# A fused causal convolution and gated feed-forward on one NeuronCore: reordering the loads and casts of the opening

## The chip, the cores and the metric

The kernel runs on one core of a Trainium2 chip. The metric is the device time of one execution in microseconds: 731.14 us is the median of three runs of the kernel before (730.99 to 731.43). The profile comes from a further execution of 730.78 us, whose profiled span is 728.7 us. All times of single instructions are counted from the start of that span.

Names used here: PE is TensorE (PEld its weight loads), DVE is VectorE, ACT is ScalarE, POOL is GpSimd, SP is SyncE, which here issues DMAs and carries a few waiting no-ops. A "q" behind a name (SPq, ACTq) is the sequencer of the engine.

## The reference: what is computed

Two steps. A causal depthwise convolution of 7 taps along the sequence, with one softmax-normalised set of taps for each of 8 heads of 24 channels; then a feed-forward layer whose activation is h cos h.

```python
def _attn_ref(x, weight):                 # x: (8, 4096, 192), weight: (8, 7)
    w = np.exp(weight - np.max(weight, axis=-1, keepdims=True))
    w = w / (np.sum(w, axis=-1, keepdims=True) + 1e-09)
    x_pad = np.concatenate([np.zeros((B, pad, D)), x], axis=1)       # pad = 6
    idx = np.arange(S)[:, None] + np.arange(K)[None, :]
    x_unf = x_pad[:, idx, :].reshape(B, S, K, H, group)
    return np.einsum('hk,bskhg->bshg', w, x_unf).reshape(B, S, D)

def _moe_ref(x, w_in, w_out):             # x: (32768, 192), w_in: (192, 2048), w_out: (2048, 192)
    h = x @ w_in
    return (h * np.cos(h)) @ w_out
```

All inputs and the output are float32; the kernel multiplies in bfloat16 and adds in float32.

## The kernel before

The 32768 tokens are 64 tiles of 512 (t = 0 to 63) and 32 units of 1024 (a unit is two tiles). A unit goes this way: load x (768 KB, and 96 KB of "edges", the rows ahead of each block of 128), cast to bf16 (GpSimd), convolve on TensorE with a band matrix, copy out of PSUM to `ct`, double it (GpSimd), turn it with a DMA transpose into `cT`, mend the edges (GpSimd). A tile then has eight steps j: `mm1` (h = w_in' cT, 4 matmuls), `gcu` (cosine on ACT, product on DVE), and matmuls `mm2_step` with w_out for tiles one and two behind. The order on each engine is written by hand.

Loads of the opening, all on the queue of SP except the tiny convolution weights:

```python
    w_f = consts.tile([128, NC, NP, 128], FP32)
    w_src = moe_w_in.rearrange("(m k) (t f) -> t m k f", k=NC, t=2)
    HP = NP // 2                                  # NP = 8, NC = 3

    def load_w(q):                                # q: half of the steps j; t: partitions 0-63 or 64-127
        for t in range(2):
            nc.sync.dma_start(out=w_f[64 * t : 64 * t + 64, :, q * HP : (q + 1) * HP, :].rearrange("p k j f -> p k (j f)"),
                              in_=w_src[t, :, :, q * HP * 128 : (q + 1) * HP * 128])

    load_unit(0, 0, NB)                           # blocks 0-3 of unit 0
    load_w(0)
    load_unit(0, NB, UB)                          # blocks 4-7 of unit 0
    load_w(1)
    load_unit(1)
    load_edges(1)
    ...
    def load_wo(q):
        return [nc.sync.dma_start(out=wo_f[:, q * HP : (q + 1) * HP, i], in_=wo_src[:, q * HP : (q + 1) * HP, i])
                for i in range(2)]
```

Casts and the band matrix. `three` deals small copies out to DVE, ACT and POOL in turn; the activation with `AF.Sin` on a scrap cell is there to load the sine table early:

```python
    keep_warm(17)                                 # matmuls on zeros
    ...
    cast_unit(0, 0, NB)                           # ACT; every other cast_unit is GpSimd's
    nc.scalar.activation(out=scrap, in_=one, func=AF.Sin)
    ...                                           # prod, diag (DVE)
    three = [nc.vector.tensor_copy, nc.scalar.copy, nc.gpsimd.tensor_copy]
    for i in range(16):
        q, rows = divmod(i, 4)
        three[i % 3](out=band[...], in_=diag[32 * q : 32 * q + 32])
    for k in range(NC):
        three[(k + 2) % 3](out=w[:, k, 0:HP], in_=w_f[:, k, 0:HP])
    cast_unit(0, NB, UB)
    for q in range(2):
        for dma in load_wo(q):                    # w_out's loads wait for the cast just above
            tc.add_manual_dep(dma.ins, bf_last[0].ins.name, sync_dep, reason="the bandwidth is for what is needed sooner")
    ...
    conv_first()                                  # unit 0, blocks 0-3: convolution, ct copies (L299)
    turn_first(0)                                 # turned by TensorE
    turn_first(1)
    cast_unit(1)
    load_unit(2)
    load_edges(2)
```

A convolution part (`conv_part`) takes two row halves on one PSUM bank; the second group of matmuls waits for a no-op on SP that waits for the first:

```python
        mm(0, 0, start=True)
        mm(2, 1, start=True)
        turn = Turn()
        turn.mark(mm(1, 0), mm(3, 1))             # a nop on SP waits for these
        yield
        turn.wait(mm(2, 0), mm(0, 1))             # these wait for the nop
        ...
```

The order of TensorE and ACT in the first two tiles (h: mm1, r: rest of unit 0's convolution, d1 d2 and c1 c2: the two groups of a convolution part, m: mm2 steps, s: gcu, e: copy of a convolution part; d and c belong to unit 1 in tile 0 and to unit 2 in tile 1):

```python
    PE_FIRST = ["h0a h0b h1 r d1 h2 d2 h3 h4 h5 h6 c1 h7 c2 p m12",
                "h0 m8 h1 m12 q h2 h3 h4 m4 d1 m8 d2 h5 m8 h6 c1 m8 c2 h7 m4 p m8"]
    ACT_FIRST = ["s0a s0b s1 s2 ed1 ed2 s3 s4 s5 s6 ec1 ec2 s7", "s0 s1 s2 s3 s4 ed1 ed2 s5 s6 ec1 ec2 P s7"]
    ...
                if (t, k) == (0, "d1"):
                    turn_unit(0, NB, UB)          # DMA transpose of unit 0, blocks 4-7
                    nc.gpsimd.tensor_copy(out=w[:, :, HP:NP], in_=w_f[:, :, HP:NP])
                    for q in range(2):
                        nc.gpsimd.tensor_copy(out=wo[:, q * HP : (q + 1) * HP], in_=wo_f[:, q * HP : (q + 1) * HP])
    ...
                if t == 1:                        # at "q"
                    turn_unit(1)
                    mend_edges(1)
    ...
        if t == 0:
            double_unit(1)
            load_unit(3)
            load_edges(3)
            cast_unit(2)
        if t == 1:
            double_unit(2)
            cast_unit(3)
```

Of the kernel before, what the change touches and what calls it, by code (L numbers as in the profile page):

```python
# [10 lines left out]
AF = mybir.ActivationFunctionType  # L11
# [5 lines left out]
def kernel(  # L17
# [8 lines left out]
    nc = tc.nc  # L26
# [15 lines left out]
    NC = D // 64  # L42
    R = G // NC
# [24 lines left out]
    def load_edges(u):  # L68
        nc.sync.dma_start(out=x_tiles[u][:, UB, :],
                          in_=xf[u * U - 8 : u * U - 8 + U, :].rearrange("(n t) d -> n t d", t=128)[:, 0:16, :])  # L70

    def load_unit(u, n0=0, n1=UB):
        if n0 == 0:
            x_tiles[u] = xin.tile([128, UB + 1, D], FP32, name="x_f")
        nc.sync.dma_start(out=x_tiles[u][:, n0:n1, :],
                          in_=xf[u * U + n0 * 128 : u * U + n1 * 128, :].rearrange("(n p) d -> p n d", p=128))


    w_f = consts.tile([128, NC, NP, 128], FP32)
    w_src = moe_w_in.rearrange("(m k) (t f) -> t m k f", k=NC, t=2)  # L80
    HP = NP // 2

    def load_w(q):
        for t in range(2):
            nc.sync.dma_start(out=w_f[64 * t : 64 * t + 64, :, q * HP : (q + 1) * HP, :].rearrange("p k j f -> p k (j f)"),  # L85
                              in_=w_src[t, :, :, q * HP * 128 : (q + 1) * HP * 128])

    load_unit(0, 0, NB)
    load_w(0)
    load_unit(0, NB, UB)  # L90
    load_w(1)
    load_unit(1)
    load_edges(1)
    wo_f = consts.tile([128, NP, 2, D], FP32)
    wo_src = moe_w_out.rearrange("(i j p) d -> p j i d", i=2, p=128)

    def load_wo(q):
        return [nc.sync.dma_start(out=wo_f[:, q * HP : (q + 1) * HP, i], in_=wo_src[:, q * HP : (q + 1) * HP, i])
                for i in range(2)]


    one = consts.tile([128, 1], FP32)
# [16 lines left out]
    scrap = consts.tile([128, 1], FP32)  # L119
# [36 lines left out]
    w = consts.tile([128, NC, NP, 128], BF16)  # L156
# [3 lines left out]
    sync_dep = mybir.DependencyInfo(mybir.DependencyClass.Sync, mybir.DependencyReason.DATA)  # L160
# [12 lines left out]
                tc.add_manual_dep(m.ins, self.nop.ins.name, sync_dep, reason="row halves on one bank")  # L173


    bf, bf_last = {}, {}

    def cast_unit(u, n0=0, n1=UB + 1):
        copy = nc.scalar.copy if u == 0 and n0 == 0 else nc.gpsimd.tensor_copy
        bf[u] = xb0 if u == 0 else xbf_pool.tile([128, UB + 1, D], BF16, name="x_bf")  # L180

        o = 1 if u == 0 else 0
        bf_last[u] = copy(out=bf[u][:, n0 + o : n1 + o, :].rearrange("p n (h k r) -> p (n h) k r", k=NC, r=R),  # L183
             in_=x_tiles[u][:, n0:n1, :].rearrange("p n (h r k) -> p (n h) k r", k=NC, r=R))
        if u and u % UPS == 0:
            nc.gpsimd.memset(bf[u][0:8, UB, :], 0.0)
        bf.pop(u - 2, None)
# [56 lines left out]
    def double_unit(u, n0=0, n1=UB + 1):  # L244
        ct = ct_tiles[u]
        nc.gpsimd.tensor_copy(out=ct[:, n0:n1, :, 1, :], in_=ct[:, n0:n1, :, 0, :])  # L246

    def turn_unit(u, n0=0, n1=UB + 1):
        ct = ct_tiles.pop(u)
        if u not in cT:  # L250
            cT[u] = cT_pool.tile([128, UB + 1, NC, 128], BF16, name="cT")
        nc.sync.dma_start_transpose(out=cT[u][:, n0:n1].rearrange("p n c k -> p (n c) k"),  # L252
                                    in_=ct[:, n0:n1].rearrange("p n c t k -> p (n c t k)"))
        cT.pop(u - 2, None)

    def mend_edges(u):

        nc.gpsimd.tensor_copy(out=cT[u][:, 0:UB, :, 0 : K - 1],  # L258
                              in_=cT[u][:, UB].rearrange("p c (n t) -> p n c t", t=16)[:, :, :, 8 : 8 + K - 1])


    cast_unit(0, 0, NB)
    nc.scalar.activation(out=scrap, in_=one, func=AF.Sin)

    prod = consts.tile([128, HQ, E, K], BF16)
    nc.vector.tensor_tensor(out=prod, in0=mask.rearrange("p (o e) k -> p o e k", o=1).to_broadcast([128, HQ, E, K]),
# [4 lines left out]
    three = [nc.vector.tensor_copy, nc.scalar.copy, nc.gpsimd.tensor_copy]  # L271
    for i in range(16):
        q, rows = divmod(i, 4)
        three[i % 3](out=band[32 * rows : 32 * rows + 32, HQ * q : HQ * (q + 1), 32 * rows : 32 * rows + E],
                     in_=diag[32 * q : 32 * q + 32])
    for k in range(NC):
        three[(k + 2) % 3](out=w[:, k, 0:HP], in_=w_f[:, k, 0:HP])
    cast_unit(0, NB, UB)
    for q in range(2):
        for dma in load_wo(q):  # L280
            tc.add_manual_dep(dma.ins, bf_last[0].ins.name, sync_dep, reason="the bandwidth is for what is needed sooner")

    ct_tiles[0] = ct_pool.tile([128, UB + 1, NC, 2, 64], BF16, name="ct")
    cT[0] = cT_pool.tile([128, UB + 1, NC, 128], BF16, name="cT")
    copies = [nc.scalar.copy, nc.vector.tensor_copy]
# [95 lines left out]
    def evac(t, b):  # L381
        if b == 0:
            o_sb[t] = opool.tile([128, NB, D], FP32, name="o_sb")
        nc.scalar.copy(o_sb[t][:, 2 * b : 2 * b + 2, :].rearrange("p s d -> p (s d)"), o_ps.pop((t, b))[:, 0 : 2 * D])  # L384

    def store(t, b0=0, b1=2):
        nc.sync.dma_start(out=out[t * T + b0 * 256 : t * T + b1 * 256, :].rearrange("(n p) d -> p n d", p=128),
                          in_=o_sb[t][:, 2 * b0 : 2 * b1, :])
# [15 lines left out]
    for t in range(NT + 2):  # L404
        u, second = divmod(t, TPU)
        cu, cc = (u + TPU, second) if t >= TPU else (1 + t, 1)
        conv = {"c": conv_part(cu, cc, ring_banks if t else o_banks) if cu < NU else iter(())}
        if t < TPU:
            conv["d"] = conv_part(cu, 0, ring_banks if t else o_banks)
        act, done, h = (ACT_ORDER if t > 1 else ACT_FIRST[t]).split(), set(), {}  # L410

        def flush():
            while act:
                k = act[0]
                need = {"P": "p", "Q": "q", "e": k[1:2] + "2"}.get(k[0], "h" + k[1:])
                if need not in done:
                    return
                act.pop(0)
                if k == "P" and 0 <= t - 1 < NT:
                    evac(t - 1, 0)  # L420
                elif k == "Q" and 0 <= t - 2 < NT:
                    evac(t - 2, 1)
                elif k[0] == "e":
                    next(conv[k[1]], None)
                elif k[0] == "s" and t < NT:
                    gcu(t, int(k[1]), h.pop(k[1:]), *HALVES[k[2:]])

        for k in (PE_ORDER if t > 1 else PE_FIRST[t]).split():
            if k[0] == "h" and t < NT:
                h[k[1:]] = mm1(t, int(k[1]), *HALVES[k[2:]])  # L430
            elif k[0] in conv:
                next(conv[k[0]], None)
                if (t, k) == (0, "d1"):
                    turn_unit(0, NB, UB)
# [3 lines that stand above are left out]
            elif k == "r":  # L438
                conv_rest()
                double_unit(0, NB, UB)  # L440
            elif k[0] == "m":
                for q in range(step, step + int(k[1:])):
                    mm2_step(q)
                step += int(k[1:])
            elif k[0] == "p":
                assert step % (2 * STEPS) == 0
            elif k[0] == "q":
                assert step % (2 * STEPS) == STEPS
            done.add(k)
            flush()  # L450

            if k == "q":
                if second == 0 and t and u + 1 < NU:
                    turn_unit(u + 1)
                    mend_edges(u + 1)
                if t == 1:
                    turn_unit(1)
                    mend_edges(1)
                if second == 0 and u + 3 < NU:
                    cast_unit(u + 3)  # L460
                if second == 1 and t > 1 and cu < NU:
                    double_unit(cu)
                if t == NT + 1:
                    store(NT - 1, 1, 2)
            if k == "p":
                if t < NT + 1 and 0 <= t - 2:
                    store(t - 2)
                if t == NT:
                    store(NT - 1, 0, 1)
                if second == 1 and u + 4 < NU:  # L470
                    load_unit(u + 4)
                    load_edges(u + 4)
# [4 lines that stand above are left out]
            cast_unit(2)  # L477
        if t == 1:
            double_unit(2)
            cast_unit(3)  # L480


# [28 lines left out]
```

## Time and profile before

| | before |
|---|---|
| time, median of 3 runs | 731.14 us |
| profiled span | 728.7 us |
| TensorE busy | 711.5 us (98%) |
| ACT, DVE, GpSimd busy | 618.1, 611.2, 151.3 us |
| two tiles in the steady part | 22.0 us |
| tile 1's first mm1 matmul starts | 30.07 us |
| tile 2's first convolution matmul starts | 46.37 us |
| HBM read and written | 31.36 and 25.17 MB |

How to read it: busy time is a sum over the whole span, and a stage of some 45 us, in which the pipeline fills, is hardly seen in it. The timeline and the busy time of short stretches show that stage. In a timeline line, the bracket gives the idle time of the engine ahead of the instruction and what released it. A DMA issued on SP shows only the time that its issue took; when its data had landed is seen from the instruction that waited for it.

### The profile page before, as it was taken

To read this page: it belongs to the slowest core of one execution; us is meant where nothing else is said; L and a number is where in the kernel's file an instruction comes from. 1 tells how busy PE (TensorE), PEld (TensorE's weight loads), DVE (VectorE), ACT (ScalarE), POOL (GpSimd) and SP (SyncE) were. 2 spreads that over 40 slices of the span, in tenths; PEclk is the share of its full clock that TensorE was granted. 3 is DMA by queue.
4 is the path that set the end of the run, shared out by engine and by line. 5 is a ranking of instruction groups with operands and counts; after the bars stand their busy time and mean duration, and the time that the engine had idled before them with its cause. 6 is when DMAs were issued, how large, how long until landed. Compare 5 with 4: busy or idle time off the path is not lost.

```text
span 728.7 us, 26373 instructions
## 1 busy us (share of the span) xinstructions
PE 711.5 (98%) x11848; PEld 531.9 (73%) x11848; DVE 611.2 (84%) x535; ACT 618.1 (85%) x782; POOL 151.3 (21%) x126
## 2 busy tenths in 40 slices
PE   6789999999999999999999999999999999999997
PEld 3467777777777777777777777777777777777776
DVE  5568888888988888888888888888888888888884
ACT  5678889888888888888888888888888988888883
POOL 4622222102222111222202222211222211221000
PEclk9899999999999999999999999999999999999999
DMA  9863445654435554445654344555454555333411
GB/s 211 192 129 104 110 95 143 143 123 111 117 89 133 143 139 105 113 95 121 143 143 106 110 104 112 142 143 106 116 111 96 144 142 122 111 76 81 85 46 66
DMA packets 184081, 86.04 MB, mean 118 GB/s; under 512 B 111648, under 2 KB 183200, under 8 KB 183968
## 3 DMA queue, kind: packets, MB, share of 16 engines
q1 hardware_dynamic: 183960, 84.36, 48.3%
q8 instruction: 92, 1.51, 0.8%
q14 instruction: 21, 0.17, 0.1%
q10 hardware_dynamic: 8, 0.00, 0.0%
HBM read 31.36 MB, written 25.17 MB: 78 GB/s over the span
## 4 chain that ended last, share of the span: by engine, by line
PE 93%; DMA 2%; POOL 2%; issue 1%; SPq 1%; ACT 0%; DVE 0%; DVEq 0%; POOLq 0%
PE o_ps L372 45%; PE h L342 44%; PE h L194 3%; DMA x_f<-in_x_dram 1%; DMA wo_f<-in_moe_w_out_dram 1%; POOL x_bf L183 1%; SPq L252 1%; PE h L372 0%; POOL wo L437 0%; ACT cs L349 0%; POOL w L435 0%; SPq L85 0%; DVE g L353 0%; DVEq L506 0%; POOL ct L246 0%
## 5 line engine op out<-in xcount | busy, mean ns | idle before, releaser
L353 DVE TENSOR_TENSOR g<-h,cs 128x1024 bf16<-128x1024 f32 (+1 forms) x513 | 603.5, 1218 | 102.3 <-ACT cs L349 97.7
L349 ACT ACTIVATE cs<-h 128x1024 bf16<-128x1024 f32 (+1 forms) x513 | 511.8, 1026 | 65.8 <-PE h L342 58.4
L372 PE MATMUL o_ps<-wo,g 64*128 64x192 bf16 x8128 | 423.7, 243 | 1.8 <-ACT ct L209 0.6
L372 PEld LDWEIGHTS <-g 64*128 64x128 bf16 x8192 | 362.1, 94 | 85.6 <-SPq L167 1.2
L342 PE MATMUL h<-cT,w 64*128 64x512 bf16 (+1 forms) x3078 | 400.9, 378 | 0.9 <-DVE cT L310 0.3
L342 PEld LDWEIGHTS <-w 64*128 64x128 bf16 x3078 | 155.6, 94 | 87.6 <-issue 4.3
L258 POOL COPY cT<-cT 128x144 bf16<-128x144 bf16 x31 | 9.5, 308 | 497.6 <-DMA cT<-ct 366.2
L183 POOL CAST x_bf<-x_f 128x1728 bf16<-128x1728 f32 (+1 forms) x32 | 80.6, 2518 | 6.9 <-DMA x_f<-in_x_dram 6.9
L209 ACT CAST ct<-h 128x432 bf16<-128x432 f32 x120 | 56.4, 522 | 29.8 <-PE h L194 28.5
L384 ACT COPY o_sb<-o_ps 128x384 f32<-128x384 f32 x127 | 60.1, 473 | 5.0 <-PE o_ps L372 5.0
L246 POOL COPY ct<-ct 128x1728 bf16<-128x1728 bf16 (+1 forms) x32 | 51.2, 1601 | 25.3 <-ACT ct L209 24.4
L194 PE MATMUL h<-x_bf,band 64*128 64x216 bf16 x480 | 43.0, 254 | 2.0 <-POOL x_bf L183 1.2
L194 PEld LDWEIGHTS <-band 64*128 64x128 bf16 (+1 forms) x512 | 22.4, 94 | 12.6 <-issue 8.7
L194 PE MATMUL o_ps<-x_bf,band 128*128 128x96 bf16 (+1 forms) x32 | 2.7, 260 | 6.4 <-POOL x_bf L183 6.4
L110 PE MATMUL o_ps<-zero 128*128 128x512 bf16 x20 | 6.5, 488 | 1.3 <-DVE zero L105 1.3
L372 PE MATMUL h<-wo,g 64*128 64x192 bf16 x64 | 5.8, 243 | 0.0
L110 PEld LDWEIGHTS <-zero 128*128 128x128 bf16 x20 | 2.1, 116 | 4.3 <-issue 1.9
L437 POOL CAST wo<-wo_f 128x1536 bf16<-128x1536 f32 x2 | 2.9, 1472 | 0.0
L209 ACT CAST ct<-o_ps 128x432 bf16<-128x432 f32 (+1 forms) x6 | 2.4, 457 | 0.3 <-PE o_ps L194 0.3
L120 ACT ACT_TABLE_LOAD x1 | 1.3, 1283 | 1.4 <-PEq L495 1.4
L384 ACT COPY o_sb<-h 128x384 f32<-128x384 f32 x1 | 0.5, 479 | 2.4 <-PE h L372 2.4
L183 ACT CAST x_bf<-x_f 128x768 bf16<-128x768 f32 x1 | 1.2, 1243 | 1.1 <-DMA x_f<-in_x_dram 1.1
(48 smaller groups left out, 28.6 us busy)
## 6 DMA issues: line engine op xcount, KB each, us to landing
out_dram<-o_sb SPq DMA_DIRECT2D x63, 384.0 KB
x_f<-in_x_dram SPq DMA_DIRECT2D x31, 768.0 KB
x_f<-in_x_dram SPq DMA_DIRECT2D x31, 96.0 KB
w_f<-in_moe_w_in_dram SPq DMA_DIRECT2D x4, 384.0 KB
wo_f<-in_moe_w_out_dram SPq DMA_DIRECT2D x4, 384.0 KB
x_f<-in_x_dram SPq DMA_DIRECT2D x2, 384.0 KB
cT<-ct SPq DMA_TRANSPOSE x32
out_dram<-o_sb SPq DMA_DIRECT2D x2, 192.0 KB
```

The lines of the kernel that those rows point to most:

```text
L110: nc.tensor.matmul(out=idle, lhsT=zero[:, 0:128], rhs=zero, start=True, stop=True)
L183: bf_last[u] = copy(out=bf[u][:, n0 + o : n1 + o, :].rearrange("p n (h k r) -> p (n h) k r", k=NC, r=R), in_=x_tiles[u][:, n0:n1, :].rearr ...
L194: return nc.tensor.matmul(out=ps[i // 2][:, 0 : (n1 - n0) * 2 * G].rearrange("p (n k i r) -> p i n k r", n=n1 - n0, k=NC, i=2)[:, i % 2], ...
L209: copy(o[:, :, 0, :], i[:, :, 0, :])
L246: nc.gpsimd.tensor_copy(out=ct[:, n0:n1, :, 1, :], in_=ct[:, n0:n1, :, 0, :])
L252: nc.sync.dma_start_transpose(out=cT[u][:, n0:n1].rearrange("p n c k -> p (n c) k"), in_=ct[:, n0:n1].rearrange("p n c t k -> p (n c t k)"))
L258: nc.gpsimd.tensor_copy(out=cT[u][:, 0:UB, :, 0 : K - 1], in_=cT[u][:, UB].rearrange("p c (n t) -> p n c t", t=16)[:, :, :, 8 : 8 + K - 1])
L342: nc.tensor.matmul(out=h[:, i, n0 * 128 : n1 * 128], lhsT=w[rows, k, j, :], rhs=c[rows, m0 + n0 : m0 + n1, k, :], start=(k == 0), stop=(k ...
L349: nc.scalar.activation(out=cs[:, :, part], in_=h[:, :, part], func=AF.Sin, bias=math.pi / 2.0, scale=1.0)
L353: nc.vector.tensor_tensor(out=g_tiles[t][:, 2 * j : 2 * j + 2, part], in0=h[:, :, part], in1=cs[:, :, part], op=ALU.mult)
L372: m = nc.tensor.matmul(out=o_ps[tt, b][:, si * D : (si + 1) * D], lhsT=g_tiles[tt][rows, f, s * 128 : (s + 1) * 128], rhs=wo[rows, f // 2, ...
L384: nc.scalar.copy(o_sb[t][:, 2 * b : 2 * b + 2, :].rearrange("p s d -> p (s d)"), o_ps.pop((t, b))[:, 0 : 2 * D])
```

## The change

It rearranges the opening and leaves what is computed, and the work of the steady part, as it is:

- The two row halves of w_in's first half are issued by two queues, SP's and ACT's.
- Unit 1 and its edges are issued ahead of w_in's second half.
- The four loads of w_out follow in the same queue at once; the explicit wait for the cast of unit 0's second half is gone.
- The scrap activation that loads the sine table stands behind ACT's band copies instead of ahead of them.
- The three casts of w_in's first half go to DVE (k = 0) and GpSimd (k = 1, 2), none to ACT.
- The cast of unit 3 stands, in GpSimd's order, between the transpose and the edge mending of unit 1 at "q" of tile 1, instead of behind the doubling of unit 2 at the end of tile 1.

Its purpose is to have what the first tiles need land and be cast in the order in which it is needed.

```diff
-    def load_w(q):
+    def load_w(q, queues):
         for t in range(2):
-            nc.sync.dma_start(out=w_f[64 * t : 64 * t + 64, ...
+            queues[t].dma_start(out=w_f[64 * t : 64 * t + 64, ...
     load_unit(0, 0, NB)
-    load_w(0)
+    load_w(0, [nc.sync, nc.scalar])
     load_unit(0, NB, UB)
-    load_w(1)
     load_unit(1)
     load_edges(1)
+    load_w(1, [nc.sync, nc.sync])
     ...
+    load_wo(0)
+    load_wo(1)
     ...
     cast_unit(0, 0, NB)
-    nc.scalar.activation(out=scrap, in_=one, func=AF.Sin)
     ...                                          # the 16 band copies
+    nc.scalar.activation(out=scrap, in_=one, func=AF.Sin)
     for k in range(NC):
-        three[(k + 2) % 3](out=w[:, k, 0:HP], in_=w_f[:, k, 0:HP])
+        three[2 if k else 0](out=w[:, k, 0:HP], in_=w_f[:, k, 0:HP])
     cast_unit(0, NB, UB)
-    for q in range(2):
-        for dma in load_wo(q):
-            tc.add_manual_dep(dma.ins, bf_last[0].ins.name, sync_dep, reason="the bandwidth is for what is needed sooner")
     ...
                 if t == 1:
                     turn_unit(1)
+                    cast_unit(3)
                     mend_edges(1)
     ...
         if t == 1:
             double_unit(2)
-            cast_unit(3)
```

More of the change, by code (lines that the diff above doesn't have):

```diff
@@ L81 @@
     HP = NP // 2
-    def load_w(q):
+    def load_w(q, queues):
         for t in range(2):
-            nc.sync.dma_start(out=w_f[64 * t : 64 * t + 64, :, q * HP : (q + 1) * HP, :].rearrange("p k j f -> p k (j f)"),
+            queues[t].dma_start(out=w_f[64 * t : 64 * t + 64, :, q * HP : (q + 1) * HP, :].rearrange("p k j f -> p k (j f)"),
                               in_=w_src[t, :, :, q * HP * 128 : (q + 1) * HP * 128])
     load_unit(0, 0, NB)
-    load_w(0)
+    load_w(0, [nc.sync, nc.scalar])
     load_unit(0, NB, UB)
-    load_w(1)
     load_unit(1)
     load_edges(1)
+    load_w(1, [nc.sync, nc.sync])
     wo_f = consts.tile([128, NP, 2, D], FP32)
@@ L97, in load_wo @@
     def load_wo(q):
-        return [nc.sync.dma_start(out=wo_f[:, q * HP : (q + 1) * HP, i], in_=wo_src[:, q * HP : (q + 1) * HP, i])
-                for i in range(2)]
+        for i in range(2):
+            nc.sync.dma_start(out=wo_f[:, q * HP : (q + 1) * HP, i], in_=wo_src[:, q * HP : (q + 1) * HP, i])
+    load_wo(0)
+    load_wo(1)
     one = consts.tile([128, 1], FP32)
@@ L173, in wait @@
                 tc.add_manual_dep(m.ins, self.nop.ins.name, sync_dep, reason="row halves on one bank")
-    bf, bf_last = {}, {}
+    bf = {}
     def cast_unit(u, n0=0, n1=UB + 1):
@@ L182, in cast_unit @@
         o = 1 if u == 0 else 0
-        bf_last[u] = copy(out=bf[u][:, n0 + o : n1 + o, :].rearrange("p n (h k r) -> p (n h) k r", k=NC, r=R),
+        copy(out=bf[u][:, n0 + o : n1 + o, :].rearrange("p n (h k r) -> p (n h) k r", k=NC, r=R),
              in_=x_tiles[u][:, n0:n1, :].rearrange("p n (h r k) -> p (n h) k r", k=NC, r=R))
```

## The prediction, made before the changed kernel ran

> **What bounds the kernel now.** I read the page first (busy shares and chain of waits), then the busy time by stretches, then the first 50 us of the timeline line by line. The page says who sets the end:
>
> ```profile
> PE 711.5 (98%) x11848; PEld 531.9 (73%) x11848; DVE 611.2 (84%) x535; ACT 618.1 (85%) x782; POOL 151.3 (21%) x126
> ...
> PE 93%; DMA 2%; POOL 2%; issue 1%; SPq 1%; ACT 0%; DVE 0%; DVEq 0%; POOLq 0%
> ```
>
> TensorE is 93% of the chain; the rest (DMA, POOL, SPq) is the opening. The stretches show where TensorE was not full. Columns: stretch, its length, busy us (count) of PE, PEld, DVE, ACT, POOL, the granted clock, the DMA share, GB/s:
>
> ```profile
> 5.10:9.00 3.90, 3.69 (x22) 1.56 (x20) 2.24 (x9) 3.76 (x8) 1.42 (x6) 1.00 0.98 219
> 13.30:20.60 7.30, 0.89 (x20) 0.83 (x20) 2.76 (x5) 1.57 (x4) 2.56 (x2) 0.92 1.11 294
> 18.00:20.30 2.30, 0.00 (x0) 0.00 (x0) 0.00 (x0) 0.00 (x0) 2.26 (x1) 0.80 1.10 326
> 30.10:46.30 16.20, 13.34 (x189) 9.18 (x187) 11.33 (x10) 11.66 (x15) 8.15 (x5) 1.00 0.55 137
> 111.00:133.00 22.00, 22.00 (x382) 16.62 (x378) 19.16 (x17) 19.39 (x26) 4.45 (x3) 1.00 0.49 122
> ```
>
> In the steady part TensorE is full (22.00 of 22 us, two tiles of 11.0 us) and DMA is half idle. Only the opening can give time. From 13.3 to 20.6 us TensorE works 0.89 us, while DMA runs without a pause (share 1.11): the opening is fed by DMA. Here is the chain of it in the timeline (start, length, engine, line, what, count, idle time before and its releaser):
>
> ```profile
> 6.33 1.28 ACT L263 ACT_TABLE_LOAD   x1
> ...
> 9.75 0.79 ACT L299 CAST ct<-o_ps 128x768 bf16<-128x768 f32 x1
> ...
> 11.42 1.23 POOL L183 CAST x_bf<-x_f 128x768 bf16<-128x768 f32 x1 [1.53 <-DMA x_f<-in_x_dram]
> ...
> 17.93 2.33 SPq L69 DMA_DIRECT2D x_f<-in_x_dram  x1
> 18.04 2.48 POOL L183 CAST x_bf<-x_f 128x1728 bf16<-128x1728 f32 x1 [5.39 <-DMA x_f<-in_x_dram]
> 20.46 0.83 POOL L246 COPY ct<-ct 128x768 bf16<-128x768 bf16 x1
> 20.57 0.54 PE L194 MATMUL o_ps<-x_bf,band 64*128 64x216 bf16 x4 [6.41 <-POOL x_bf L183]
> ...
> 21.32 4.03 SPq L252 DMA_TRANSPOSE cT<-ct  x1
> ```
>
> The reader should see: unit 1 landed at 18.04, GpSimd cast it until 20.5, and the first convolution matmul of unit 1 (d1 in the order string) held the in-order TensorE for 6.41 us. A second, smaller hole is at the start of tile 2, where the cast of unit 3 stands last in GpSimd's order:
>
> ```profile
> 46.37 0.36 PE L194 MATMUL h<-x_bf,band 64*128 64x216 bf16 x4 [1.17 <-POOL x_bf L183]
> ```
>
> [...] Each w_in transfer writes 64 partitions, [...] 219 GB/s in 5.1 to 9.0, where w_in fills most of the traffic, against 326 GB/s in 18.0 to 20.3, where all traffic writes 128 partitions. [...]
>
> **Part 1, unit 1 ahead of w_in's second half.** Before unit 1 the queue holds 384 KB x 6 (two half units, four w_in parts); after, 384 KB x 4. At 219 GB/s the 786 KB moved back are 3.6 us. The tail matters as well: w_out was held until 12.68 us and then took bandwidth beside unit 1; now it stands behind unit 1 in the same queue. Traffic up to unit 1 and its edges is 4 x 0.393 + 0.885 = 2.46 MB. At 245 to 300 GB/s (between the two measured rates) from 2.1 us on, it ends at 10.3 to 12.1; with half a us to the semaphore, about 11.7 instead of 18.0. GpSimd's 2.5 us cast then ends at 14.2 instead of 20.5, about when TensorE, at 14.15, gets there. So d1 moves from 20.57 to **about 14.2 (-6.4)**, and the hole is gone. The clock fell to half at 19.7 after this hole; there ACT's cosine (1.02 us each) was the slower anyway (4 h-matmul pairs, 0.85 us at half clock), so I count nothing for the clock.
>
> **Part 2, second queue and table load.** [...] On ACT the five band copies (1.35 us) come before the 1.28 + 0.2 us table load and the w cast (0.62 us) goes to GpSimd; but the warm-up matmuls hold TensorE until 8.28 us, and the first ct copy on ACT (9.75) still stands behind bands and table: cast ends about 6.5, bands 7.9, table 9.4. So ct starts at 9.4: **-0.4**, which only moves the wait in front of d1.
>
> **Part 3, what gives it back.** The matmuls of d2 wait for a no-op on SP that stands, in SP's order, behind the issue of w_out, unit 2 and its edges. These issues are slowed by a full queue. I counted packets: when unit 2's edges had been issued (17.93 + 2.33 = 20.26), 6144 packets had been issued and 4527 moved, a backlog of 1617. After the change the SP queue has 192 packets fewer (w_in's half on ACT): 5952 - 1617 = 4335 must have moved, which is all up to w_in (2752) and 1583 of w_out's 2048. With w_in's second half moved at 11.3 + 3.65 = 15.0, and 326 GB/s / 768 B = 0.42 packets per ns, that is 15.0 + 3.7 = **18.7**. So d2 starts at about 18.8 instead of 22.16: 3.4 earlier, not 6.4. GpSimd needs about as long for w's second half (unit 0's doubling at 15.8, 0.83, then 1.47 us: 18.1). From d2 on ACT paces: two ct copies 0.94, four cosines 4.27, two copies 0.94, the first of these freeing w_out's bank. Before, d2 to tile 1's first matmul took 22.16 to 30.07 = 7.9, of which ACT's s2 took some; after, 18.8 + 6.5 = **25.3**.
>
> The transpose of unit 0's second half must have landed by then too. Before, issued at 21.32, its packets ended near 27.4, some 2.1 us after unit 2's last. Unit 2's transfer ends about 1 us earlier at best (all the traffic ahead of it is the same in bytes), near 24.1 to 25.0, so the transpose lands at 24.9 (6.1 us after an issue at 18.8) to 26.4. I take tile 1's start as **25.6 against 30.07: -4.5**.
>
> **Part 4, cast of unit 3 ahead of unit 1's edge mending.** In tile 1 GpSimd was idle for 7.12 us waiting for the transpose; the cast (2.5 us) fits into it, if unit 3 has landed. It takes away the 1.17 us hole at tile 2: **-1.2**. The work on TensorE, DVE and ACT after that is unchanged, so the shift reaches the end whole.
>
> Sum: -4.5 - 1.2 = -5.7 from 731.14 gives 725.4; I round towards the smaller gain, **725.8**.
>
> **Rivals.** (a) *The full -7.6*: if d2 isn't held by SP and the transpose lands early, tile 1 starts at 23.3 and the end is 723.3 or a little under. For it speaks that GpSimd and ACT would allow it; against it the measured backlog. (b) *Hidden anyway*: total traffic through unit 2 and the transpose is what counts, the order of it is not. Then tile 1 moves by the 1 us of the faster w_in at most, and with the 1.2 us of part 4 the end is 729. For it speaks a DMA share of 1.0 throughout; against it that tile 1 started 2.7 us after the transpose had landed. (c) *A new wait*: the cast of unit 3 now stands before unit 1's edge mending; if unit 3 lands late, the mending and tile 2 move back. Unit 3 is issued after the transpose, about 24, and needs 4.8 us (27.64 to 32.5 before): 28.8, cast by 32, the mending due at about 37. Unlikely; it would put the end at 727 to 730. (d) Unit 0 lands later [...]: at most 0.5 us at the front, swallowed by the wait before d1.
>
> **Range and chances.** From (a) to (b), with a margin: 722.8 to 728.8. A 2% gain would be 14.6 us, twice the whole hole; a 2% loss would need a wait of 14.6 us that nothing in the order suggests. So within 2% at 0.98.
>
> **What would show it.** Unit 1's cast starting near 11.7 and d1 near 14.2; the clock not falling, or later; SP's issue of unit 2's edges ending near 18.7 and d2 right after; the transpose landing at 25 to 26 with tile 1's first matmul released by it or by ACT; no idle of TensorE on the cast of unit 3. The prediction is wrong if unit 1 lands after 13 (then the queues' rate was mis-sized), if d2 starts well before 18 (the backlog rule fails) or if the shift is lost before 70 us because tile 1 gets longer than its 15.7 us.

## The result, and the profile after

The changed kernel takes 726.97 us (median of four runs, 726.2 to 727.4) against 731.28 us for the kernel before: a ratio of 0.9939, 95% interval 0.9922 to 0.9957. That is 4.3 us less; 5.3 us had been predicted (725.8, range 722.8 to 728.8), and a change within 2%, which it is.

The page of the changed kernel, busy shares and chain by engine:

```profile
PE 711.8 (98%) x11848; PEld 531.5 (73%) x11848; DVE 611.2 (84%) x535; ACT 618.0 (85%) x781; POOL 151.9 (21%) x127
...
PE 95%; DMA 2%; DVE 1%; ACT 1%; SPq 1%; POOL 0%; DVEq 0%; issue 0%; POOLq 0%
```

The engines' work is what it was, and TensorE's part of the chain has grown from 93% to 95%: what went is waiting. The timeline of the changed kernel shows where (start, length, engine, line, what, count, idle time before and its releaser; its convolution is L198 where it was L194 before, the cast L187 where it was L183):

```profile
14.40 2.49 POOL L187 CAST x_bf<-x_f 128x1728 bf16<-128x1728 f32 x1 [1.88 <-DMA x_f<-in_x_dram]
...
16.95 0.36 PE L198 MATMUL o_ps<-x_bf,band 64*128 64x216 bf16 x4 [2.34 <-POOL x_bf L187]
...
18.06 1.98 SPq L69 DMA_DIRECT2D x_f<-in_x_dram  x1
...
20.16 0.54 PE L198 MATMUL o_ps<-x_bf,band 64*128 64x216 bf16 x4 [2.20 <-SPq L171]
...
27.26 0.99 PE L372 MATMUL o_ps<-wo,g 64*128 64x192 bf16 x10 [0.61 <-ACT ct L213]
...
28.02 0.39 PE L342 MATMUL h<-cT,w 64*128 64x512 bf16 x1
```

Unit 1's cast starts at 14.40 instead of 18.04, so d1 runs at 16.95 instead of 20.57 (3.6 earlier) after an idle time of 2.34 us instead of 6.41. But then d2, at 20.16 instead of 22.16, has a new wait of 2.20 us: it is released by a no-op of SP (L171), and SP was issuing unit 2's edges until 18.06 + 1.98 = 20.04. Tile 1 begins at 28.02 instead of 30.07, so 2.05 of the 3.6 us are left. In the kernel before, the same two instructions were:

```profile
22.16 0.59 PE L194 MATMUL o_ps<-x_bf,band 64*128 64x216 bf16 x4
...
30.07 0.39 PE L342 MATMUL h<-cT,w 64*128 64x512 bf16 x1
```

The rest of the gain is at tile 2, whose first convolution matmuls are at 42.99 instead of 46.37 and wait for nothing. By stretches (length, busy us and count of PE, PEld, DVE, ACT, POOL, clock, DMA share, GB/s), the changed kernel from tile 2 on:

```profile
44.30:66.30 22.00, 22.00 (x374) 16.81 (x371) 18.86 (x17) 19.41 (x26) 4.63 (x4) 1.00 0.50 123
```

The kernel before had 21.93 us in its 22 us from 46.30 on. From there the kernels are alike, and the shift reaches the end: 3.4 us at tile 2, and 3.3 between the two profiled spans (728.7 and 725.4). The medians differ by 4.3, as the profiled execution of the changed kernel, 727.11 us, was one of its longer ones.

### The profile page after: what moved, and what is told of

Its sections match the earlier page's. It is cut to its first block, busy times and chain, and to the rows that moved or that the text cites. A ratio compares the mean times of both kernels' runs of the same rounds, so it can differ in the third digit from the quotient of the medians.

```text
span 725.4 us, 26371 instructions
## 1 busy us (share of the span) xinstructions
PE 711.8 (98%) x11848; PEld 531.5 (73%) x11848; DVE 611.2 (84%) x535; ACT 618.0 (85%) x781; POOL 151.9 (21%) x127
## 4 chain that ended last, share of the span: by engine, by line
PE 95%; DMA 2%; DVE 1%; ACT 1%; SPq 1%; POOL 0%; DVEq 0%; issue 0%; POOLq 0%
PE o_ps L372 46%; PE h L342 45%; PE h L198 3%; DMA x_f<-in_x_dram 2%; DVE g L353 1%; ACT cs L349 0%; PE h L372 0%; POOL x_bf L187 0%; SPq L69 0%; SPq L75 0%; DVEq L506 0%; ACT o_sb L384 0%; PE o_ps L198 0%; POOL ct L250 0%; ACT ct L213 0%
## 5 line engine op out<-in xcount | busy, mean ns | idle before, releaser
L187 POOL CAST x_bf<-x_f 128x1728 bf16<-128x1728 f32 (+1 forms) x32 | 80.4, 2515 | 2.0 <-DMA x_f<-in_x_dram 1.9
L198 PE MATMUL h<-x_bf,band 64*128 64x216 bf16 x480 | 43.0, 254 | 0.8 <-DVE g L353 0.5
L198 PEld LDWEIGHTS <-band 64*128 64x128 bf16 (+1 forms) x512 | 22.2, 94 | 9.5 <-SPq L171 3.3
L198 PE MATMUL o_ps<-x_bf,band 128*128 128x96 bf16 (+1 forms) x32 | 2.5, 245 | 4.5 <-POOL x_bf L187 2.3
```

The lines of the kernel that those rows point to most:

```text
L198: return nc.tensor.matmul(out=ps[i // 2][:, 0 : (n1 - n0) * 2 * G].rearrange("p (n k i r) -> p i n k r", n=n1 - n0, k=NC, i=2)[:, i % 2], ...
```

## The experiments

All are compared with the kernel before on the same chip in the same job. Where two variants are compared with each other, the difference of their medians is given together with their ranges or intervals; variants of different jobs are best compared by their ratios. Packet times come from the packet records of the traces and are counted from the start of the span, like all others.

**The changed kernel again**, as the yardstick of the first job.

> The changed kernel once more, as the yardstick for the three beside it. Both theories: 4 to 5 us under the kernel before (727.0 against 731.3), d1 released by the cast of unit 1 near 17.0 us, d2 released by a no-op of SP near 20.2 us, tile 1's first mm1 matmul near 28.0 us. If the warm-up of the clock is what varies from run to run, the end of the warm-up matmuls may lie at 8.3 instead of 9.4 us.

Measured: 726.54 us (725.58 to 726.83), ratio 0.9934, interval 0.992 to 0.9947; d1 at 16.80, d2 at 18.82, tile 1 at 26.72, the warm-up matmuls' end at 8.67. TensorE's timeline:

```profile
16.80 0.54 PE L198 MATMUL o_ps<-x_bf,band 64*128 64x216 bf16 x4 [2.21 <-DVE ct L213]
...
18.82 0.54 PE L198 MATMUL o_ps<-x_bf,band 64*128 64x216 bf16 x4 [0.19 <-SPq L171]
...
22.84 0.82 PE L342 MATMUL h<-cT,w 64*128 64x512 bf16 x6 [1.02 <-DVE g L353]
```

The gain stands, but not all that was expected of the opening. Unit 1's cast ended at 16.65, and what released d1 was DVE's copy of unit 0 out of the same PSUM banks (`ct`). SP was done with unit 2's edges at 18.70 instead of 20.04, so its no-op held d2 for only 0.19 us instead of 2.20. The opening's single times scatter by more than 1 us from run to run (d2 at 20.16 and 18.82), so below one profile alone decides nothing smaller than that.

**The cast of unit 3 at its old place.**

```diff
                 if t == 1:
                     turn_unit(1)
-                    cast_unit(3)
                     mend_edges(1)
...
         if t == 1:
             double_unit(2)
+            cast_unit(3)
```

> The changed kernel with the cast of unit 3 back at its old place at the end of tile 1. Theory (the hole at tile 2 is a loss of its own): the 1.17 us idle of TensorE on this cast comes back and the time is 1.2 us above the changed kernel, near 728.2. Rival (the hole only took up slack that another wait would have filled): less than 0.4 us. Tile 1's start stays at 28.0 us in both.

Measured: 728.13 us (727.73 to 728.87), ratio 0.9958 (0.9945 to 0.997), 1.6 us above the yardstick, no single run overlapping. Its timeline has the hole of the kernel before again, to the hundredth:

```profile
43.75 0.36 PE L198 MATMUL h<-x_bf,band 64*128 64x216 bf16 x4 [1.17 <-POOL x_bf L187]
```

This part of the change is worth 1.2 to 1.6 us by itself.

**One queue for w_in's first half.**

```diff
-    load_w(0, [nc.sync, nc.scalar])
+    load_w(0, [nc.sync, nc.sync])
```

> The changed kernel with both row halves of w_in's first half on SP's queue again. Theory (the second queue gains nothing[...]): w's casts start within 0.5 us of the changed kernel's 9.9 to 10.0, unit 1's cast within 0.5 us of 14.4, time within 0.5 us. Rival [...]: w lands 1 us later, unit 1's cast starts near 15.4, time 1 us longer.

Measured: 727.88 us (727.25 to 728.79), ratio 0.9956 (0.9943 to 0.9968): 1.3 us above the yardstick, again without overlap of single runs. So the second queue gains, as the rival had it, but not because w_in lands earlier. GpSimd's timeline in this variant:

```profile
9.62 1.40 POOL L281 CAST w<-w_f 128x512 bf16<-128x512 f32 x2 [2.15 <-DMA w_f<-in_moe_w_in_dram]
...
15.29 2.49 POOL L187 CAST x_bf<-x_f 128x1728 bf16<-128x1728 f32 x1 [3.10 <-DMA x_f<-in_x_dram]
```

w_in's first half lands no later than with two queues (9.62 against 10.00), but unit 1 does (15.29 against 14.40, which is within the scatter of single profiles). What all engines do and what DMA moves from 2.1 to 10.1 us, the changed kernel first, then this variant (columns as above):

```profile
2.10:10.10 8.00, 7.94 (x45) 3.41 (x44) 3.91 (x15) 5.68 (x12) 4.25 (x13) 1.00 0.98 244
2.10:10.10 8.00, 7.46 (x54) 3.45 (x52) 4.27 (x16) 5.68 (x12) 4.63 (x13) 1.00 0.91 223
```

DMA moves 9% more with two queues, 244 against 223 GB/s. In the same stretch the other ten profiles with two queues have 235 to 261, and the other two with one queue (the kernel before and the order alone, below) 223 and 230.

**Unit 2's load behind the transpose.**

```diff
     cast_unit(1)
-    load_unit(2)
-    load_edges(2)
...
                 if (t, k) == (0, "d1"):
                     turn_unit(0, NB, UB)
+                    load_unit(2)
+                    load_edges(2)
```

> The changed kernel with unit 2's load and its edges issued behind the transpose of unit 0, so that SP reaches d1's no-op without the slowed issue of unit 2. Theory (d2 is held by SP's issue): d2 follows h2 at about 18.0 us instead of 20.16, the transpose is issued at 17.8 instead of 20.24, tile 1 starts at 25.9 instead of 28.0, time 2 us under the changed kernel, near 725. Rival (total traffic sets tile 1's start: w_out lands only near 23 us and the mm2 matmuls need its cast, or the transpose comes no earlier): d2 moves but tile 1 starts within 0.7 us of 28.0, time within 0.7 us.

Measured: 725.46 us (724.82 to 726.12), ratio 0.9922 (0.991 to 0.9935), 1.1 us under the yardstick, though single runs overlap. TensorE's timeline in this variant:

```profile
17.95 0.36 PE L198 MATMUL o_ps<-x_bf,band 64*128 64x216 bf16 x4 [2.57 <-POOL x_bf L187]
18.13 0.83 PE L340 MATMUL h<-cT,w 64*128 64x512 bf16 x6
18.77 0.36 PE L198 MATMUL o_ps<-x_bf,band 64*128 64x216 bf16 x4
18.96 1.43 PE L340 MATMUL h<-cT,w 64*128 64x512 bf16 x6
20.80 1.46 PE L340 MATMUL h<-cT,w 64*128 64x512 bf16 x6 [0.41 <-POOL w L435]
```

d2 (18.77) follows d1 by 0.82 us and without a wait; in the changed kernel it was 3.21 us. What held it was SP's issue of unit 2. The gain is half of what was expected. Two things in the profiles go with that: the next wait is close behind, as the fifth step (20.80) needs w_in's second half, whose cast ends at 20.7; and the wait for SP was not always 2.20 us (0.19 in the yardstick's profile). Everything in this profile began late, the warm-up matmuls ending at 10.15 us, and tile 1 starts at 27.02, after the yardstick's 26.72. So the gain itself rests on the timed runs.

**TensorE kept busy in the two waits of tile 0.**

```diff
+                if (t, k) in ((0, "d1"), (0, "d2")):
+                    if k == "d1":
+                        warm = h_pool.tile([128, 2, T], FP32, name="h")
+                    for _ in range(11 if k == "d1" else 10):
+                        nc.tensor.matmul(out=warm[:, 0, :], lhsT=zero[:, 0:128], rhs=zero, start=True, stop=True)
                 next(conv[k[0]], None)
```

> The changed kernel with matmuls on zeros, into an unused PSUM buffer, ahead of d1 (11) and ahead of d2 (10), so that TensorE is not idle in the two waits of tile 0. Theory (the half clock that follows the waits sets the pace of tile 0's later steps: six matmuls of one step take three times 427 ns = 1.28 us at half clock, more than ACT's 1.02): the clock stays at full, ACT's cosines follow each other every 1.02 us, tile 1 starts about 1 us earlier against d2, time 1 us under the changed kernel, near 725.6. Rival (the prediction's: ACT paces these steps, the clock costs nothing): time within 0.4 us of the changed kernel. In both d1 and d2 must not start later than the wait that releases them.

Measured: 727.03 us (725.95 to 727.6), ratio 0.994 (0.9927 to 0.9952): no gain. The clock did stay at full throughout (in the changed kernel it was at half from 18.18 to 25.00 us), and ACT's timeline shows what this does to the cosines. The changed kernel first, then this variant:

```profile
22.02 1.02 ACT L349 ACTIVATE cs<-h 128x1024 bf16<-128x1024 f32 x1 [0.34 <-PE h L342]
23.30 1.02 ACT L349 ACTIVATE cs<-h 128x1024 bf16<-128x1024 f32 x1 [0.26 <-PE h L342]
24.58 1.96 ACT L349 ACTIVATE cs<-h 128x1024 bf16<-128x1024 f32 x2 [0.26 <-PE h L342]
```

```profile
21.10 2.88 ACT L349 ACTIVATE cs<-h 128x1024 bf16<-128x1024 f32 x3
```

At half clock they start 1.28 us apart, each waiting for TensorE; at full clock three take 2.88 us back to back. From d2 to tile 1 it is 7.09 us (19.87 to 26.96) instead of 7.86. That the clock alone makes this difference isn't shown: in the yardstick's profile it was back at full at 20.15, three cosines took 2.86 us back to back there too, and yet from d2 to tile 1 it was 7.90. At full clock another wait comes up, in the yardstick (line 22.84 above) and here:

```profile
23.45 0.82 PE L342 MATMUL h<-cT,w 64*128 64x512 bf16 x6 [1.28 <-DVE g L353]
```

The seventh step needs one of the three PSUM buffers of `h`, which DVE's product of the fourth step frees, and DVE takes 4.62 us for four products. The timed runs show no gain at all, as the two intervals overlap almost wholly. What the clock is worth for the whole stays open; an estimate from the width of these intervals is below about 1 us.

**w_in's second half and w_out held until unit 1 is cast.**

```diff
-    load_w(1, [nc.sync, nc.sync])         # and load_wo(0), load_wo(1)
...
     cast_unit(1)
+    for dma in [*load_w(1, [nc.sync, nc.sync]), *load_wo(0), *load_wo(1)]:
+        tc.add_manual_dep(dma.ins, bf_last[1].ins.name, sync_dep, reason="held until unit 1 is cast")
```

> The changed kernel with w_in's second half and w_out held back until unit 1 has been cast; only the landing of unit 1 is of interest, the time will be longer (up to 735 us). Measured so far: 2150 of the 2176 packets of units 0 and 1 have started at 10.3 to 10.5 us, yet unit 1's cast starts at 13.7 to 15.4. Theory ([...] it would be there without w_in's second half): unit 1's cast starts at 13 us or later. Rival (the tail comes from the packets of w_in's second half[...]): with those held back the cast starts by 12 us.

Measured: one run of 732.24 us. Timeline of GpSimd and TensorE:

```profile
12.80 2.52 POOL L184 CAST x_bf<-x_f 128x1728 bf16<-128x1728 f32 x1 [1.00 <-DMA x_f<-in_x_dram]
...
15.84 0.36 PE L195 MATMUL o_ps<-x_bf,band 64*128 64x216 bf16 x4 [2.21 <-DVE ct L210]
```

12.80 lies between the two expectations, and the packet records decide in the main for the rival. (In them the 2150th of the 2176 packets of units 0 and 1 starts at 11.6 us or later in every kernel, not at 10.3 to 10.5 as the expectation has it.) In this variant the 2150th starts at 11.80, the last at 12.14, and the cast 0.66 us after it. In the changed kernel it is 12.01, 13.34 and 1.06 us more, in the yardstick 11.86, 13.00 and 1.14. So with nothing behind them unit 1's last packets come about 1 us earlier and count as landed sooner. The instruction packets of the traces (16 KB each, 92 with a mean of 1.02 us in the changed kernel) have no part in it: the earliest in the span of any of these traces is at 16.1 us (18.19 in the changed kernel), when unit 1 had landed.

And the second line shows a wait that the expectation did not have: with unit 1 cast by 15.3, d1 still didn't start before 15.84, since its PSUM banks are those of unit 0's second half, which DVE copies out (ct) behind its products, as in the yardstick.

**The order of the loads alone**, in the kernel before.

```diff
-    load_w(1)
     load_unit(1)
     load_edges(1)
+    load_w(1)
...                                       # w_out's four loads next in the queue, no wait for the cast
```

> The kernel before with one part of the change alone: unit 1 and its edges ahead of w_in's second half, and w_out behind it in the same queue. One queue, the table load ahead of the band copies and the late cast of unit 3 as before. Theory (the parts add up: the changed kernel 4.5 us under before, of which the cast of unit 3 is 1.6 and the second queue 1.3): this part alone gives 1.6 us, time near 729.5, unit 1's cast at 15 us, tile 1 at 29.6. Rival (the order alone is hidden, as total traffic sets tile 1's start): within 0.5 us of the kernel before. Rival (order is all of the gain in tile 1): 3 us, near 728.

Measured: 729.65 us (median of 21 runs), ratio 0.9976, interval 0.9969 to 0.9982: 1.8 us (1.3 to 2.3 by the interval), as the sum of the parts had it. Unit 1's cast starts at 14.93, d1 at 17.48, d2 waits for SP until 21.43, tile 1 at 29.27.

**Unit 2 later, and TensorE kept busy ahead of d1.**

```diff
+                    load_unit(2)                  # behind turn_unit(0, NB, UB), as above
+                    load_edges(2)
+                    for _ in range(11 if k == "d1" else 0):
+                        nc.tensor.matmul(out=warm[:, 0, :], lhsT=zero[:, 0:128], rhs=zero, start=True, stop=True)
```

> Unit 2's load behind the transpose, and 11 matmuls on zeros ahead of d1. Theory: the gains of both add up, 1.1 us for the first as measured and up to 1 us for the second: near 724.5, faster than every kernel so far. Rival (with the wait for SP gone the idle time is too short to lower the clock for long, so there is nothing left to gain): within 0.4 us of 725.5.

Measured: 725.04 us (724.72 to 727.14), ratio 0.992 (0.9907 to 0.9933). It can't be told from unit 2's load alone. In the profiled run unit 1 landed only at 16.7 us, the latest of all variants.

**Table load and casts as before.** The sine table ahead of the band copies, one of the three w casts on ACT.

```diff
     cast_unit(0, 0, NB)
+    nc.scalar.activation(out=scrap, in_=one, func=AF.Sin)
...
-    nc.scalar.activation(out=scrap, in_=one, func=AF.Sin)
-        three[2 if k else 0](out=w[:, k, 0:HP], in_=w_f[:, k, 0:HP])
+        three[(k + 2) % 3](out=w[:, k, 0:HP], in_=w_f[:, k, 0:HP])
```

> The changed kernel with two of its parts undone: the sine table load ahead of ACT's band copies again, and the three casts of w_in's first half dealt to DVE, ACT and GpSimd as before. Theory (this part only moves the wait in front of d1, which ends with the landing and the cast of unit 1): d1 stays within the scatter of 16.4 to 17.0 us, time within 0.5 us of the changed kernel, near 726.7. Rival (ACT's earlier start carries through to the end): the time is 1 us longer, near 727.7.

Measured: 725.7 us (725.16 to 727.28), ratio 0.9925 (0.9911 to 0.9938), against 0.9934 (0.992 to 0.9947). Undoing this part costs nothing; whether it even gains 0.8 us these runs don't separate. In its profile d1 was as late as 18.31, outside the expected 16.4 to 17.0: the w cast on ACT waited for its data until 10.36 and kept back ACT's first ct copy (10.88), and in the end DVE's ct copy released d1. Yet d2, at 19.88, came between the 18.82 and 20.16 of the changed kernel's two profiles, as SP's no-op held it in any case (0.56 us here).

**Unit 2 later, and w_in's second half and w_out held until w_in's first half is cast.**

```diff
-    load_w(1, [nc.sync, nc.sync])         # and load_wo(0), load_wo(1); unit 2's load as above
...
     for k in range(NC):
-        three[2 if k else 0](out=w[:, k, 0:HP], in_=w_f[:, k, 0:HP])
+        last_w = three[2 if k else 0](out=w[:, k, 0:HP], in_=w_f[:, k, 0:HP])
+    for dma in [*load_w(1, [nc.sync, nc.sync]), *load_wo(0), *load_wo(1)]:
+        tc.add_manual_dep(dma.ins, last_w.ins.name, sync_dep, reason="held until w_in's first half is cast")
```

> Unit 2's load behind the transpose (as in e4_unit2_later), and w_in's second half and w_out held until w_in's first half is cast (about 11 us). Theory (part of unit 1's tail comes from these packets, as in e6_held): unit 1's cast starts at 12.8 to 13.2 us instead of 14.1 to 15.4, d1 at about 15.8, and since w's second half still lands near 17 us, the time is 0.5 to 1 us under e4_unit2_later's 725.5. Rival (the bytes held back are missed later: w_out lands a microsecond later and its cast holds the first mm2 matmul): time at or above 725.5.

Measured: 724.82 us (724.37 to 725.27), ratio 0.9911 (0.9899 to 0.9923): the lowest median, 1.7 us under the changed kernel's yardstick and 6.5 us under the kernel before. Unit 1's cast started at 13.41. d1 came at 17.03, not 15.8: as in the held variant and the yardstick it was released by DVE's copy of unit 0. Tile 1 began at 26.16. From unit 2's load alone (724.82 to 726.12) it can't be told.

**Unit 2 later, and w_in's second half by two queues too.**

```diff
-    load_w(1, [nc.sync, nc.sync])
+    load_w(1, [nc.sync, nc.scalar], (0,))          # row half 0, where it was
...
     nc.scalar.activation(out=scrap, in_=one, func=AF.Sin)
+    load_w(1, [nc.sync, nc.scalar], (1,))          # row half 1, on ACT's queue
```

> Unit 2's load behind the transpose (as in e4_unit2_later), and the second row half of w_in's second half on ACT's queue too, issued behind the table load at about 9.5 us. Theory [...]: w's second half and w_out land about 1 us earlier, time up to 1 us under e4_unit2_later's 725.5. Rival (its packets now run beside the tail of unit 1 and lengthen it, or its issue holds ACT's first ct copy): d1 later by up to 1 us, time at or above 725.5.

Measured: 725.67 us (724.87 to 725.89), ratio 0.992 (0.9908 to 0.9932): as unit 2's load alone. The last packet of w_in's second half started at 17.77 us, against 18.02 with unit 2's load alone, its cast at 18.70 against 19.27, and the cast of w_out's second half at 23.64 against 23.75. So the last loads came no earlier than the scatter of such times. For the first half it had been 244 against 223 GB/s from 2.1 to 10.1 us, as shown above.

**The held version, d1 and d2 on the ring of PSUM buffers.**

```diff
-            conv["d"] = conv_part(cu, 0, ring_banks if t else o_banks)
+            conv["d"] = conv_part(cu, 0, ring_banks)
```

> e9_held_w with the first convolution part of unit 1 (d1, d2) on the ring of three PSUM buffers instead of the two banks that DVE's copies of unit 0 (ct) free only at 16.7 us. Theory (a bank held by DVE was a second wait in front of d1, hidden behind the first): d1 is released by the cast of unit 1 again and starts at about 16.0 instead of 17.0, but w_in's second half still lands near 18.4 us and holds the fourth step, so the time stays within 0.5 us of e9_held_w's 724.8. Rival (d1 is all that counts in tile 0): 1 us shorter, 723.8. Rival (the ring now runs short and h2 waits for DVE): longer than 725.3.

Measured: 725.34 us (724.28 to 726.7), ratio 0.992 (0.9906 to 0.9933), not distinguishable from the held version. TensorE's timeline:

```profile
15.62 0.36 PE L195 MATMUL h<-x_bf,band 64*128 64x216 bf16 x4 [1.41 <-POOL x_bf L184]
...
19.34 1.03 PE L339 MATMUL h<-cT,w 64*128 64x512 bf16 x7 [1.88 <-POOL w L434]
```

d1 is released by the cast again and 1.4 us earlier than in the held version; the idle time turns up at the fifth step, which waits for the cast of w_in's second half.

## Why the prediction was right, and where its working failed

The four parts, each measured by undoing it or doing it alone, add up: order of the loads 1.8, second queue 1.3, cast of unit 3 1.6, table load and casts none, together 4.7 against the 4.5 of the yardstick's job. The sum agrees better than the runs can tell, as three of the parts are known to within about 1 us only. Step by step:

- **What bounds it** and that only the opening could give: right. So was the carry of the shift to the end: from tile 1's start to tile 2's it took 14.97 us, against 16.30 with the hole.
- **Part 1**, d1 at 14.2: it was 16.95. The amount was right: the 2.46 MB up to unit 1's edges had been moved at 11.66 us, within the predicted 10.3 to 12.1. The step's two rates, 219 and 326 GB/s, were measured; that the number of partitions makes the difference between them was not shown. What failed is that the step took the queue for one line, in which unit 1 has landed half a us after that (the author's estimate; with the loads behind it held, the cast came 0.55 to 0.66 us after the start of the last packet). The first packet of w_in's second half started at 10.96, and 191 of them (0.39 MB) before unit 1's last one, at 13.34; the cast followed 1.06 us later, at 14.40 instead of 11.7. With the loads behind it held, it was 12.14 and 12.80. So the prediction's own sign of being wrong came true (unit 1 after 13), but for another reason than the rate. The step had a second hole: it took d1's only wait to be the cast, though DVE's copies held its banks until 16.67. The yardstick's profile, that with the table load first and the two with the loads held and d1 on those banks show the bank as the releaser.
- **Part 2**: that a faster w_in is worth 1 us at most, as rival (b) has it, was the author's estimate. With the second queue DMA moved 9% more (244 against 223 GB/s from 2.1 to 10.1 us, beside loads of all 128 partitions), and the gain in time was 1.3 us, a little above the 1 us. For the table load, -0.4 that moves only a wait, the end is right. The ct copy began at 10.09, not 9.4, because the warm-up matmuls ended at 9.38 instead of 8.28.
- **Part 3**, SP's queue: the mechanism was right (no-op of SP as releaser, and moving unit 2 away removes the wait). The size was off, 18.7 predicted and 20.04 measured. The backlog (packets issued but not started) at the end of the issue was not far off in this profile: 1488, against 1548 in the kernel before, where the prediction counted 1617. What was mis-sized is how soon the packets moved: the 4335th started at 19.74 us instead of 18.7. A fixed backlog is no rule either, as it was 1934 in the yardstick and 1577 and 1646 in the two variants with one queue. The yardstick's 18.70 is the predicted time, but by luck: there the 4335th packet started at 19.44.
- **From d2 to tile 1**, 6.5 predicted: it was 7.86, and 7.90 in the yardstick. The step let ACT set the pace alone. It counted a mm1 as four pairs, 0.85 us at half clock, where it is six matmuls in three pairs (three k, two row halves; four, in the section on the kernel, is wrong): 3 x 427 ns = 1.28 us, longer than ACT's cosine (1.02 us). And it left out DVE, whose product frees the PSUM buffer of a later step: the seventh step waited 1.02 and 1.28 us for it where the clock was full. So 6.5 was too short either way, with 7.09 the shortest measured. That the half clock cost time in the whole isn't shown. (In the kernel before it fell at 19.37, not 19.7.)
- **Part 4**, -1.2: 1.17 in the profile, 1.6 in the timed runs.
- **Rivals**: (a) fell, as no profile has tile 1 before 25.2, and SP held d2 (2.20 us, 0.19 in the yardstick). (b) fell, as tile 1 moved by more than 1 us and was released by ACT's copy and not by the transpose. (c) did not happen, and of (d) there was 0.1 us (unit 0's cast at 5.17 instead of 5.07).

So the total lay in the range because the losses were looked for in the right places, and with some luck: that d1 came 2.75 us later than predicted can have cost little, since SP's no-op held d2 until 20.09 us anyway. Tile 1 was credited with 4.5 us and got 2.05 in the profile (3.35 in the yardstick's).

What stays open is why unit 1's cast starts 1.1 to 1.3 us after the start of its last packet when other loads are behind it (the seven profiles in which the packets can be told apart), and only 0.55 to 0.66 us after it when they are held (three).

## What to carry to other kernels

Move a load forward for the instruction that waits for it, and then list every other thing that instruction needs: here the data, the PSUM bank and a no-op on the issuing engine were three waits within 3 us, and removing one paid for only a part of itself each time. Keep an engine's queue free of issues that can stall when it also carries waits of the compute engines: here SP's issues of unit 2 and its edges took 3.57 and 1.98 us, and d2 waited 2.20 us for the no-op behind them. A gain in an opening is only real at the first instruction of the steady part, so measure it there.

## What the runs showed of the hardware

- Two transfers into the two halves of the partitions, beside loads of 128 partitions: from 2.1 to 10.1 us DMA moved 235 to 261 GB/s in eleven profiles with the two on two queues, and 223 to 230 in three with both on one.
- Transfers of one queue overlap. The first packet of w_in's second half started 2.4 us before unit 1's last one, which stood ahead of it in the queue (10.96 and 13.34 us in the changed kernel). Holding the loads behind it brought unit 1's cast to 12.80, 13.04 and 13.41 us in three profiles; in the ten with w_in's second half behind it, it lay between 13.73 and 16.73.
- SP's issue of a load of 768 KB took 3.57 us when 2104 packets issued on SP before it had not started (unit 2 in the changed kernel, at 14.45 us), and 0.39 us when all had (unit 3 in the kernel before, at 27.64 us; the last of them started at 27.36).
- The 17 warm-up matmuls, the same in all kernels, took 4.81 to 6.25 us. In every trace single ones took some 630 ns up to a certain time and some 380 ns from then on, and the record of the full clock begins there: at 5.23 us with the loads held until unit 1 is cast (4.81 us), at 7.94 in the changed kernel (6.15), at 8.81 with unit 2's load behind the transpose (6.25).
